# Transposing the third batch's q and k by DMA in place of TensorE

## Chip, cores, metric

One core of one Trainium2 chip. The metric is device time in microseconds (us) of one launch; the runs of the kernel before lie within 0.3% (316.71 to 317.66 us).

## The reference, cut to what matters

Sliding-window attention (window 32 to each side, 8 batches of 8 heads, 576 positions, head size 64), then a feed-forward layer with a smooth ReLU over all 4,608 positions.

```python
scores = scale * np.matmul(q, k.transpose(0, 1, 3, 2))      # q, k: [8, 8, 576, 64] float32
scores = np.where(np.abs(pos[:, None] - pos[None, :]) <= 32, scores, -1e9)
attn = softmax(scores); x = attn @ v                        # heads joined: [4608, 512]
h = x @ w_in; g = smelu(h); out = g @ w_out                 # 512 -> 2048 -> 512
```

## The kernel before

The kernel's score matmuls read q and k with the head's 64 values on the partitions (the lines `bb<-qT,kT 64*64` in the profiles), so each batch's q and k are transposed. The kernel has two ways. The first two batches after the start (numbers 1 and 2 in the code; number 2 is called the third batch below) are loaded in long runs and transposed by TensorE into PSUM, from where ACT and DVE copy them out. The later batches are loaded in natural rows of 64 values and transposed by one DMA per tensor, issued from SyncE.

```python
LONG = 3                       # batches 0..2 go through TensorE, 3..7 through DMA transposes
def load_rows(b, t):           # one DMA of 576 KB, runs of 1152 bytes at the destination
    x = nat.tile([128, NU, 2, D], BF, name=nm, tag=nm)           # pool "nat": two buffers a tag
    nc.gpsimd.dma_start(out=dst[b], in_=src[b].rearrange("(m e) (p j) d -> (e p) m (j d)", e=2, j=9))
def load_nat(b, t):            # two DMAs of 288 KB, runs of 128 bytes at the destination
    for h in range(2):
        nc.gpsimd.dma_start(out=x[:, :, h], in_=src[b, NY * h:NY * h + NY]...)
def tposes(b, *sets):          # TensorE: 36 transposes a tensor into the PSUM pairs "bb" ...
    for (t, half), pool in zip(sets, (ps_s, ps_n)):
        tp = pool.tile([128, 2, 8, 128], BF, name="tp", tag="bb")
        todo += [tpose(b, 2 * half + part, t, (A.copy, V.tensor_copy)[part], tp[:, part]) for part in range(2)]
    for copy in todo:          # ... and four copies out by ACT and DVE
        copy()
def xpose(b, t):               # DMA transpose
    nc.sync.dma_start_transpose(out=qkT(b, t)..., in_=(qn, kn)[t][b]...)
# [...]  loads are all issued on GpSimd, in order, as early as buffers allow:
put([(load_rows, 2, t) for t in range(2)] + [(load_v, 2, n) for n in range(4)])
# [...]  the slots
for n, a in enumerate((18, 20, 22, 27)):            at(a, seq[2 + n][0])    # sums
for n, a in enumerate((13.5, 14.5, 16, 18, 20, 25, 27)): at(a, seq[n][1])   # scores; n = 5: batch 2
for b, *a in ((1, 11.5, 12.5), (2, 19.5, 21.5)):    # slots of the TensorE transposes
    for t in range(2):
        at(a[t], (tposes, b, (t, 0), (t, 1)))
for b in range(LONG, B):                            # later batches: loads, then DMA transposes
    a = sl[5 * (b - 1) - 7] - 17
    ...
# [...]  one slot of the main loop:
#   hp (8 matmuls), ACT rr, DVE mx and gT;  run(a);  matmuls into op of an earlier tile;  run(a + 0.5);
#   then on SyncE the DMA transposes that are placed in this slot. Output stores are on SyncE too.
```

The softmax here doesn't subtract the row's maximum and nothing guards it: scores larger than these inputs give would overflow.

## Time and profile before

| | before |
|---|---|
| time, median | 316.87 us (316.71 to 317.66; three runs, a fourth makes it 316.85) |
| PE, DVE, ACT busy | 95%, 80%, 61% |
| DMA engines | busy 90% or more until about 110 us |

A line of the timeline is: start in us, duration in us, engine, source line, operation, written and read tiles, count; in brackets, the idle time of the engine before it and what ended it. The prediction below shows the lines of before and reads them. Its packet rates are in the packets' records of the same trace: about 840 packets of 256 bytes per us while a DMA transpose runs in quiet (414 to 427 per half us from 83.5 to 85.5 us), 84 to 92 long load packets per half us from 46.5 to 50 us, and 603 to 617 short ones from 59.5 to 62.5 us. The record of 219 to 220 ns that it names is that of one TensorE transpose.

### The profile page before, as it was taken

The numbers are of one execution on the slowest core, as the hardware profiler recorded it, in microseconds if no ns is written. First come the engines' busy times: TensorE is split into PE (matmuls) and PEld (weight loads), VectorE is DVE, ScalarE is ACT, GpSimd is POOL, SyncE is SP. The second block draws the span as 40 slices with busy tenths as digits, with TensorE's granted clock in tenths as the row PEclk, the third lists the DMA queues.
The fourth block names the chain that finished last, engine by engine and source line by source line (L and its number), as shares of the span: only waits on it lengthen the run. The fifth ranks groups of instructions, "written<-read, shape, count | busy, mean of one in ns | idle before, by whom it ended". The sixth has DMA issues, their size and how long they took to land.

```text
span 315.0 us, 8563 instructions
## 1 busy us (share of the span) xinstructions
PE 298.4 (95%) x3670; PEld 207.7 (66%) x3707; DVE 250.8 (80%) x393; ACT 192.1 (61%) x316; POOL 69.5 (22%) x83
## 2 busy tenths in 40 slices
PE   8987998999999999999999999999999999999995
PEld 3566877776666666666666666666666666667652
DVE  4279986877988888888888888888888888878760
ACT  3677375765765776567756666566676666654431
POOL 8784354652060406040503000000000000000000
PEclk9999999999999999999999999999999999999999
DMA  9999999999999969997993983005501100100111
GB/s 151 185 199 202 174 215 174 164 169 166 168 167 117 107 141 167 101 91 123 173 127 54 90 127 95 33 35 111 108 35 35 36 33 35 36 33 35 42 60 67
DMA packets 123558, 34.54 MB, mean 110 GB/s; under 512 B 108160, under 2 KB 119168, under 8 KB 123520
## 3 DMA queue, kind: packets, MB, share of 16 engines
q0 software_dynamic: 94176, 18.06, 74.1%
q1 hardware_dynamic: 29200, 15.63, 19.7%
q8 instruction: 29, 0.48, 0.6%
q10 hardware_dynamic: 144, 0.29, 0.4%
q14 instruction: 9, 0.07, 0.1%
HBM read 36.70 MB, written 9.44 MB: 146 GB/s over the span
## 4 chain that ended last, share of the span: by engine, by line
PE 86%; DVE 5%; ACT 5%; issue 3%; ACTq 0%
PE hp L484 37%; PE op L424 35%; PE bb L289 5%; PE op L440 4%; PE bb L223 2%; PE z L332 2%; DVE mx L490 2%; ACT pt L231 1%; ACT rc L296 1%; DVE gT L491 1%; PE tp L183 1%; DVE xT L301 1%; ACT lr L295 1%; DVE kT L186 1%; DVE qT L186 1%
## 5 line engine op out<-in xcount | busy, mean ns | idle before, releaser
L484 PE MATMUL hp<-xT,w_in 128*128 128x256 bf16 x1152 | 149.3, 273 | 4.0 <-DVE mx L490 1.9
L488 ACT ACTIVATE rr<-hp 128x512 f32<-128x512 f32 x144 | 85.7, 595 | 92.5 <-PE hp L484 91.1
L484 PEld LDWEIGHTS <-w_in 128*128 128x128 bf16 x1152 | 111.8, 98 | 44.2 <-issue 5.0
L424 PE MATMUL op<-w_out,gT 128*128 128x512 bf16 x477 | 123.0, 379 | 5.0 <-issue 4.8
L490 DVE TENSOR_TENSOR mx<-hp,rr 128x512 f32<-128x512 f32 x144 | 99.3, 690 | 33.7 <-ACT rr L488 31.5
L491 DVE SCALAR_TENSOR_TENSOR gT<-rr,mx 128x512 bf16<-128x512 f32 x144 | 99.6, 692 | 4.9
L424 PEld LDWEIGHTS <-gT 128*128 128x128 bf16 x512 | 47.6, 98 | 36.7
L231 ACT ACTIVATE pt<-bb 128x1024 bf16<-128x1024 f32 (+1 forms) x33 | 33.2, 1012 | 5.4 <-PE bb L223 4.0
L105 POOL DMA_DIRECT2D vn<-in_v_dram x32 | 27.3, 867 | 40.7 <-PE bb L223 36.2
L301 DVE TENSOR_TENSOR xT<-bb,rc 128x512 bf16<-128x512 f32 (+1 forms) x32 | 21.1, 658 | 11.1 <-ACT rc L296 10.4
L429 ACT COPY osb<-op 128x512 f32<-128x512 f32 x32 | 18.7, 583 | 11.5 <-PE op L424 11.1
L296 ACT ACTIVATE rc<-lr 128x512 f32<-128x512 f32 (+2 forms) x40 | 23.6, 589 | 1.3
L295 ACT ACTIVATE lr<-bb 128x512 f32<-128x512 f32 (+2 forms) x40 | 22.0, 551 | 0.8 <-PE bb L289 0.7
L97 POOL DMA_DIRECT2D qn<-in_q_dram x10 | 12.2, 1222 | 43.9 <-DMA qT<-qn 37.5
L289 PE MATMUL bb<-pt,ones 64*64 64x256 bf16 (+3 forms) x352 | 19.6, 255 | 1.9 <-DVE kT L186 0.8
L197 DVE TENSOR_TENSOR pt<-pt,mask 128x1024 bf16<-128x1024 bf16 (+1 forms) x34 | 21.0, 616 | 0.2 <-ACT pt L231 0.2
L289 PE MATMUL bb<-pt,vn 64*64 64x128 bf16 (+3 forms) x712 | 18.5, 204 | 0.2 <-issue 0.2
L289 PEld LDWEIGHTS <-ones 64*64 64x64 bf16 x352 | 10.4, 105 | 10.4 <-issue 10.4
L289 PEld LDWEIGHTS <-vn 64*64 64x64 bf16 x712 | 16.8, 107 | 0.3 <-issue 0.3
L440 PE MATMUL op<-w_out,gT 128*128 128x256 bf16 x128 | 16.3, 273 | 0.0
L97 POOL DMA_DIRECT2D kn<-in_k_dram x10 | 12.1, 1213 | 9.7 <-PE tp L183 3.9
L440 PEld LDWEIGHTS <-gT 128*128 128x128 bf16 x128 | 12.1, 98 | 1.7
(53 smaller groups left out, 107.8 us busy)
## 6 DMA issues: line engine op xcount, KB each, us to landing
out_dram<-osb SPq DMA_DIRECT2D x36, 256.0 KB, 2.3
vn<-in_v_dram POOLq DMA_DIRECT2D x32, 144.0 KB, 8.2
qn<-in_q_dram POOLq DMA_DIRECT2D x10, 288.0 KB, 7.7
kn<-in_k_dram POOLq DMA_DIRECT2D x10, 288.0 KB, 8.8
w_out<-in_moe_w_out_dram POOLq DMA_DIRECT2D x4, 512.0 KB, 13.2
qn<-in_q_dram POOLq DMA_DIRECT2D x2, 576.0 KB, 14.7
kn<-in_k_dram POOLq DMA_DIRECT2D x2, 576.0 KB, 15.7
w_in<-in_moe_w_in_dram POOLq DMA_DIRECT2D x8, 128.0 KB, 5.4
```

The costliest lines, as they stand in the source:

```text
L97: nc.gpsimd.dma_start(out=x[:, :, h], in_=src[b, NY * h:NY * h + NY].rearrange("y s d -> (y s) d") .rearrange("(u p) d -> p u d", p=128))
L105: nc.gpsimd.dma_start(out=vn[b][64 * a:64 * a + 64, :, h], in_=v[b, y:y + 2].rearrange("y s d -> (y s) d") .rearrange("(c r) d -> r c d", ...
L231: A.activation(p, ps[:, :, :128 * n].rearrange(like, y=m), AF.Exp, scale=D ** -0.5)
L289: nc.tensor.matmul(bb[HD[h], a, o + c0:o + c1], ones[HD[a]] if c is None else vn[b][HD[a], c, h], p(a, h), start=n == 0, stop=True, skip_g ...
L295: A.activation(lr[:, :, :D0], bb[:, :, D0:2 * D0], AF.Ln)
L296: A.activation(rc[:, :, :D0], lr[:, :, :D0], AF.Exp, scale=-1.0)
L424: nc.tensor.matmul(o, gT[tt // 2][:, j, 128 * (tt % 2):128 * (tt % 2) + 128], w_out[:, j], start=not done, stop=len(done) == 2 * NF - 1, s ...
L440: nc.tensor.matmul(o[:, tt], gT[p][:, j, 128 * tt:128 * tt + 128], w_out[:, j, 256 * half:256 * half + 256], start=not done, stop=len(done ...
L484: nc.tensor.matmul(hp[:, j], w_in[:, kk, 256 * f + 128 * j:256 * f + 128 * j + 128], xT[:, kk, r0:r0 + TB], start=n == 0, stop=n == 3)
L488: A.activation(rr, hp, AF.Relu, scale=0.5, bias=0.5)
L490: V.tensor_max(mx, hp, rr)
L491: V.scalar_tensor_tensor(gT[t][:, 2 * f:2 * f + 2], rr, 1.0, mx, op0=ALU.min, op1=ALU.mult)
```

## The change

The intent: 72 matmuls, their eight copies and two waits leave the busiest engine's row, and the DMA engines do the work instead, as they do for the later batches.

```diff
-    LONG = 3
+    LONG = 2
@@
-    put([(load_rows, 2, t) for t in range(2)] + [(load_v, 2, n) for n in range(4)])
+    put([(load_nat, 2, t) for t in range(2)] + [(load_v, 2, n) for n in range(4)])
@@
-    for b, *a in ((1, 11.5, 12.5), (2, 19.5, 21.5)):
-        for t in range(2):
-            at(a[t], (tposes, b, (t, 0), (t, 1)))
-    loads, xps = {}, {}
-    for b in range(LONG, B):
+    for t, a in enumerate((11.5, 12.5)):
+        at(a, (tposes, 1, (t, 0), (t, 1)))
+    loads, xps = {}, {17: [(2, 0)], 18: [(2, 1)]}
+    for b in range(LONG + 1, B):
```

## The prediction

> **What bounds the kernel now.** I read the page's busy shares and chain first: TensorE (PE) is busy 95% of the 315.0 us, and the chain that ended last is PE work for 86% of the span.
>
> ```profile
> PE 298.4 (95%) x3670; PEld 207.7 (66%) x3707; DVE 250.8 (80%) x393; ACT 192.1 (61%) x316; POOL 69.5 (22%) x83
> DMA  9999999999999969997993983005501100100111
> PE 86%; DVE 5%; ACT 5%; issue 3%; ACTq 0%
> ```
>
> So time is saved only by taking work out of PE's row, or the few waits inside it. The line in the middle (DMA, busy tenths in 40 slices) says that the transfers are busy in nearly all of the first third (a slice is 7.9 us, 9 is 90% or more), which is where the change adds transfers. Next I read the PE timeline around the work that goes. A "slot" is one turn of the main loop; each begins with eight matmuls of L484, so slots can be counted: 17 starts at 52.85 us, 19 at 57.25, 20 at 60.22, 22 at 66.54, 25 at 73.14.
>
> ```profile
> 58.12 1.04 PE L440 MATMUL op<-w_out,gT 128*128 128x256 bf16 x8
> 59.09 1.20 PE L183 MATMUL tp<-ident,qn 128*64 128x128 bf16 x36
> 60.22 1.05 PE L484 MATMUL hp<-xT,w_in 128*128 128x256 bf16 x8
> 62.03 0.30 PE L289 MATMUL bb<-pt,ones 64*64 64x256 bf16 x4 [0.77 <-DVE qT L186]
> ...
> 65.42 1.20 PE L183 MATMUL tp<-ident,kn 128*64 128x128 bf16 x36
> 66.54 1.05 PE L484 MATMUL hp<-xT,w_in 128*128 128x256 bf16 x8
> 68.36 0.28 PE L289 MATMUL bb<-pt,ones 64*64 64x192 bf16 x4 [0.77 <-DVE kT L186]
> ...
> 74.11 0.42 PE L223 MATMUL bb<-qT,kT 64*64 64x128 bf16 x16
> ```
>
> The second and fifth lines are the third batch's transposes (slots 19 and 21). Each is followed, one slot later, by a PE idle gap of 0.77 us: the sums need the PSUM pair "bb" that the transposes have filled, until DVE has copied it out. The last line is slot 25's scores, the first reader of the third batch's qT and kT: the deadline for whatever makes them.
>
> The deadline is then held against the transfers. The loads as they are, then an existing later transpose pair (fourth batch) and its landing:
>
> ```profile
> L91 POOL DMA_DIRECT2D qn<-in_q_dram x1: 754/754/754, 33.4 to 33.4; - x1
> DMA to landing us min/median/max: 15.9/15.9/15.9
> ...
> L91 POOL DMA_DIRECT2D kn<-in_k_dram x1: 742/742/742, 36.3 to 36.3; - x1
> DMA to landing us min/median/max: 15.8/15.8/15.8
> ```
>
> ```profile
> 40.30 32.29 SPq L446 DMA_DIRECT2D out_dram<-osb  x4
> 81.44 0.34 SPq L430 DMA_DIRECT2D out_dram<-osb  x1
> 81.96 2.89 SPq L190 DMA_TRANSPOSE qT<-qn  x1
> 85.01 2.41 SPq L190 DMA_TRANSPOSE kT<-kn  x1
> ```
>
> So q lands at 33.4 + 15.9 = 49.3 us and k at 36.3 + 15.8 = 52.1, and in a quiet stretch SyncE is occupied for 2.4 to 2.9 us by each transpose; the view of issues gives 4.9 us to landing for q and 4.7 for k.
>
> [...] 840 packets of 256 bytes per us while one runs, 215 GB/s. [...] here a record is 219 to 220 ns, but 36 issue in 1.13 us, 31 ns each, and that is what PE's row loses. [...] a 256 KB store issued at 52.9 us, amid loads, gets its first packet only at 57 us, and then loads fall from about 610 packets per half us to 130 to 200 beside the store's 95 to 99.
>
> **Removed.** 72 matmuls with 72 weight loads, in two runs: 60.22 - 59.09 = 1.13 us and 66.54 - 65.42 = 1.12 us of PE's row. The two PE waits after them, 2 x 0.77 = 1.54 us. Eight copies out of PSUM: DVE 4 x 0.72 = 2.9 us and ACT 4 x 0.76 = 3.0 us, beside PE and worth nothing more than the waits already counted. Sum on PE's row: 1.13 + 1.12 + 1.54 = 3.8 us.
>
> Does another wait step into the gap? The freed sums of slot 20 also need the earlier use of "bb" to be multiplied out by DVE, done at 59.4 us; without the transposes they are due at 59.1 + 0.9 = 60.0, so that holds. Stepping ACT's and DVE's order through slots 20 to 22 with their recorded durations, the next sums would be due at about 64.3 us, and their inputs at about 63.3; they stand at 68.36 now. That gives 4.0 us, the upper figure; I take 3.8.
>
> **Added: loads.** The third batch's q and k become four loads of 288 KB, in runs of 128 bytes at the destination, in place of two of 576 KB in runs of 1,152. From the packets' records in the saturated stretch: 90 long packets per half us, so 512 take 2.9 us; 610 short ones, so 2,304 take 1.9 us and a tensor (4,608) 3.8 us, 4.2 to 4.4 by the landings of the fourth batch. Extra: about 1.4 us per tensor, 2.8 us for both. The number of packets grows ninefold, but DMA time does not. In the program's order each load waits for the one eight before it; from the old landings I get q complete at about 51 us and k at about 55, and the values after them at about 60, needed in slot 27 (after 77 us now).
>
> **Added: transposes.** Two on SyncE, placed after the store at 52.87. q can start at about 53.3, k at about 56.2 (its load being in at 55). In quiet, landing would be 58 and 61 us. The stretch is not quiet: as with the store, about 3.5 us before the first packet, and then, at half of the 840 packets per us, 2,304 take 5.5 us. Estimated q lands at 62 to 63 and k at 67 to 68. The reader in slot 25, now at 74.1, will come at 74.1 - 3.8 = 70.3. So the transposes are hidden, with 2 us to spare in the slow case and 9 in the quiet one. No PE, DVE or ACT time is added. SyncE's next store is held up some us; its three output buffers bear that. The fifth batch's loads now wait for these transposes rather than for PE's; that moves them by a few us at most, and the transposes that use them run near 113 us.
>
> **Moved.** Everything after slot 22 moves forward by the same amount, if nothing later is tied to a transfer: the fourth batch's q and k have landed by 66 us and are transposed after 82, so there is room to lose the added 2.8 us and more.
>
> **Rivals.** (1) The transposes land late: amid saturated loads they take longer than I sized, and slot 25 waits. For it: the store's 7 us to landing there against 2.3 in the median. Against: 9 us of slack in quiet. It would give back what exceeds 70.3 us; k at 72 leaves 2 us of gain (315), at 75 none (317.5). (2) DVE or ACT becomes the bound where PE's row closes up, so that the gain is cut to the PE time alone, 2.25 us (314.6). For: DVE is busy 3.6 of the 4 us from 58 us on. Against: 1.35 us of that is a pair of the copies which go. (3) The extra load time pushes a later load past its need. Against it: the room above. It would cost 1 to 3 us. (4) Removing PE work moves the end by nothing, because transfers bound the stretch. Against: between 57 and 71 us the view of waits names a transfer only once on PE's side, for 0.2 us, at a weight load that goes.
>
> **Range and chances.** 316.87 - 3.8 = 313.1. The low end is the 4.0 us of the stepping plus some small luck, 312.2; the high end is the first rival with about 2.5 us given back, 315.4. Faster by over 2% needs 6.3 us, two thirds more than all that is removed: 0.02. Slower by over 2% needs the kernel to stall for 10 us at slot 25, beyond anything seen of HW transfers here: 0.03. The rest, 0.95, is within 2%.
>
> **What would show it.** In the trace after: no L183 lines with qn or kn after 45 us, 72 in place of 144 of them; no 0.77 us gaps at L289 with qT or kT copies as releasers; sums of slot 22 near 64.3 to 64.6 us; two DMA_TRANSPOSE on SyncE near 53 and 56 us, landing under 68; the L223 group of slot 25 without a wait for a transfer, near 70.3 us; the fifth batch's loads still well ahead. I am wrong if that group waits for a DMA_TRANSPOSE (rival 1), if new L484 or L289 waits for DVE stand between 58 and 70 us (rival 2), if a later load ends a PE wait (3), or if slot 25 starts earlier and the end does not (a later bound that I missed).

## The result, and the profile after

The changed kernel took 318.98 us in the median (318.45 to 319.50, four runs) against 316.85 (316.71 to 317.66) of the kernel before. The ratio is 1.0062 (95% interval 1.0037 to 1.0087). Ratios here are the mean time of one kernel's runs over the mean of the other's runs of the same rounds, so not quite the ratio of the medians. Timed again later beside other experiments (e9_again), it took 317.89 us, ratio 1.0035 (1.0007 to 1.0063). So it is one to two us slower, within 2% as forecast but outside the range of 312.2 to 315.4 us, and on the other side of the kernel before.

The page of the kernel after, its busy line, its clock and the chain by engine and by line:

```profile
PE 303.3 (96%) x3635; PEld 206.5 (65%) x3635; DVE 247.9 (78%) x388; ACT 189.1 (60%) x312; POOL 72.7 (23%) x85
PEclk9999999997999999999999999999999999999999
PE 75%; DMA 18%; POOL 4%; issue 1%; ACT 0%; POOLq 0%
```

PE has 35 fewer records: 72 matmuls are gone, but the trace before lacks 37 records, 35 of them of its L424 (477 of 512, 123.0 us busy against 131.3 here), so PE's busy times of the two pages can't be compared. One slice of the clock shows a 7. The chain now contains 18% of DMA, where the kernel before had none among its leading entries. Where that is, the timeline of PE in the kernel after tells:

```profile
58.94 1.04 PE L439 MATMUL op<-w_out,gT 128*128 128x256 bf16 x8
59.81 1.04 PE L483 MATMUL hp<-xT,w_in 128*128 128x256 bf16 x8
60.78 0.30 PE L289 MATMUL bb<-pt,ones 64*64 64x256 bf16 x4
...
65.03 0.28 PE L289 MATMUL bb<-pt,ones 64*64 64x192 bf16 x4
...
69.82 1.04 PE L483 MATMUL hp<-xT,w_in 128*128 128x256 bf16 x8
74.31 0.42 PE L223 MATMUL bb<-qT,kT 64*64 64x128 bf16 x16 [3.45 <-DMA kT<-kn]
74.66 1.47 PE L423 MATMUL op<-w_out,gT 128*128 128x512 bf16 x4
75.92 1.91 PE L483 MATMUL hp<-xT,w_in 128*128 128x256 bf16 x8
77.62 1.49 PE L423 MATMUL op<-w_out,gT 128*128 128x512 bf16 x4
78.95 1.04 PE L483 MATMUL hp<-xT,w_in 128*128 128x256 bf16 x8
```

The transposes and both 0.77 us gaps are gone: slot 22's sums start at 65.03 instead of 68.36 us. Then the scores of slot 25, ready to go just after 70.8 us, wait 3.45 us for kT. After the wait the same groups of matmuls take longer: 1.91 us for eight of L483 that take 1.04 elsewhere. The view by windows of the kernel after (start and end, length, busy us of each engine with instructions, granted PE clock, DMA share, GB/s) gives the reason:

```profile
70.00:74.00 4.00, 0.86 (x8) 0.52 (x6) 2.56 (x4) 0.60 (x1) 1.22 (x1) 1.00 1.78 167
74.00:76.00 2.00, 1.69 (x21) 0.81 (x22) 0.16 (x1) 1.02 (x1) 1.19 (x1) 0.78 1.43 258
76.00:78.00 2.00, 2.00 (x10) 1.29 (x9) 0.53 (x1) 0.08 (x1) 0.02 (x1) 0.50 2.43 155
78.00:80.00 2.00, 2.00 (x16) 1.16 (x18) 1.38 (x2) 0.51 (x1) 1.56 (x2) 0.86 2.51 158
```

The clock falls to a half (0.50). Its records put this from 75.13 us for 3.41 us, so about 1.7 us of work are lost. SyncE's timeline in the kernel after shows how kT came so late:

```profile
53.68 0.38 SPq L445 DMA_DIRECT2D out_dram<-osb  x1
54.18 7.29 SPq L190 DMA_TRANSPOSE qT<-qn  x1
61.57 6.81 SPq L190 DMA_TRANSPOSE kT<-kn  x1
```

Each transpose holds SyncE for about 7 us, not the 2.4 to 2.9 us of the quiet ones (nine of ten in the kernel before; one took 3.5), and the second is issued only when the first lets go. By the packets' records, q's 2,304 packets run from 59.53 to 65.96 us and k's from 66.81 to 72.95, at about 412 per us for most of that time, with an equal number of load packets beside them; the loads alone move about 1,200 per us. When SyncE lets go of q's transpose, at 61.47 us, only 633 of its packets have gone out: the hold is long, but it doesn't last for the whole transfer. kT has landed at 74.27 us.

To compare the traces slot by slot I take the start of DVE's last operation (gT) in each slot. Up to slot 19 the executions differ by -0.21 to +1.35 us against the profiled run of before, in most of them set before the first slot ends. The changed kernel stands at +0.82 in its first profile (its clock rose to full at 6.86 us, that of before at 5.18, and the 14 fillers at the start took 5.98 us against 5.15), +0.35 in its second, and at -0.19 and -0.21 in two experiments that share its early instructions (e6_early, e7_swap), so this belongs to the execution, and I subtract what slot 19 has. The end varies too: before and e1_none end 9.9 us after the last slot's gT starts, the other nine traces 10.3, with PE's last matmul at the same distance in all. From slot 19 on:

| us against before, less the difference in slot 19 | by slot 24 | by slot 27 | by slot 48 and to the last slot |
|---|---|---|---|
| changed kernel | -4.14 | +1.06 | +1.18 |

So 4.14 us were gained, and 5.20 lost again in two slots: 3.45 of waiting and about 1.75 of slow clock.

### The profile page after: what moved, and what is told of

Read it like the earlier page. It is cut to its first block, busy times and chain, and to the rows that moved or that the text cites.

```text
span 317.4 us, 8453 instructions
## 1 busy us (share of the span) xinstructions
PE 303.3 (96%) x3635; PEld 206.5 (65%) x3635; DVE 247.9 (78%) x388; ACT 189.1 (60%) x312; POOL 72.7 (23%) x85
## 4 chain that ended last, share of the span: by engine, by line
PE 75%; DMA 18%; POOL 4%; issue 1%; ACT 0%; POOLq 0%
PE op L423 36%; PE hp L483 33%; DMA kn<-in_k_dram 12%; PE bb L289 5%; DMA kT<-kn 4%; DMA qh<-in_q_dram 2%; PE bb L223 2%; POOL w_in L109 2%; POOL vn L105 1%; POOL w_out L114 1%; POOL qn L97 0%; POOL kh L84 0%; POOL qn L91 0%; ACT osb L428 0%; PE bb L248 0%
## 5 line engine op out<-in xcount | busy, mean ns | idle before, releaser
L483 PE MATMUL hp<-xT,w_in 128*128 128x256 bf16 x1152 | 150.1, 274 | 3.7 <-DVE mx L489 1.3
L483 PEld LDWEIGHTS <-w_in 128*128 128x128 bf16 x1152 | 112.4, 98 | 44.4 <-issue 5.1
L423 PE MATMUL op<-w_out,gT 128*128 128x512 bf16 x512 | 131.3, 382 | 0.0
L423 PEld LDWEIGHTS <-gT 128*128 128x128 bf16 x512 | 47.8, 98 | 37.2 <-issue 0.6
L97 POOL DMA_DIRECT2D qn<-in_q_dram x12 | 14.6, 1219 | 52.6 <-DMA qT<-qn 46.0
L97 POOL DMA_DIRECT2D kn<-in_k_dram x12 | 14.5, 1217 | 11.1 <-DMA kn<-in_k_dram 6.8
L223 PE MATMUL bb<-qT,kT 64*64 64x128 bf16 x520 | 13.0, 217 | 3.6 <-DMA kT<-kn 3.5
L289 PEld LDWEIGHTS <-ones 64*64 64x64 bf16 x352 | 10.3, 105 | 9.0 <-issue 8.9
```

Source lines behind the costliest of these rows:

```text
L289: nc.tensor.matmul(bb[HD[h], a, o + c0:o + c1], ones[HD[a]] if c is None else vn[b][HD[a], c, h], p(a, h), start=n == 0, stop=True, skip_g ...
L423: nc.tensor.matmul(o, gT[tt // 2][:, j, 128 * (tt % 2):128 * (tt % 2) + 128], w_out[:, j], start=not done, stop=len(done) == 2 * NF - 1, s ...
L483: nc.tensor.matmul(hp[:, j], w_in[:, kk, 256 * f + 128 * j:256 * f + 128 * j + 128], xT[:, kk, r0:r0 + TB], start=n == 0, stop=n == 3)
```

## The experiments

**Theory:** the gain on PE is real (4.1 us). kT is late because, beside saturated loads, a transpose gets every second packet (about 412 per us, to 412 of the loads), and the two run one after the other; and the wait for it costs more than its length, because the clock drops. **Rivals:** the load of k in small packets is what makes it late; or the cost lies elsewhere (packets, other engines) and the wait is only where it shows. The first rival is not idle, since the chain of waits of the kernel after, in order of time, reads:

```profile
39.22 14.47 DMA kn<-in_k_dram
...
54.38 7.19 DMA kn<-in_k_dram
61.57 12.70 DMA kT<-kn
74.31 0.42 PE bb L223 x16
```

It leads from kT to a load of kn. But the load that was issued at 54.38 us belongs to the fourth batch, and the third batch's k was in at 55.2 us (40.4 plus 14.8 by the view of its tile).

One thing stays open: none of the experiments tells whether the transposes run one after the other because SyncE is held or because packets keep their order in SyncE's queue. The packets speak for the queue. In the kernel before, k's transpose was issued at 85.01 us, while q's packets were going out, and its first packet came at 86.24, when q's last went; in the changed kernel only 0.85 us lie between q's last packet and k's first, and the hold can't have cost more if that order is kept.

### e1_none: no transposes at all

```diff
+    for t in range(2):
+        P.memset(qkT(2, t), 0.0)
-    loads, xps = {}, {17: [(2, 0)], 18: [(2, 1)]}
+    loads, xps = {}, {}
```

> Wrong result on purpose: the changed kernel, with the third batch's two DMA transposes left out and its qT and kT set to zero by GpSimd early. Loads as in the changed kernel. Theory (the loss comes from the wait of 3.45 us for kT in slot 25 and the lowered PE clock after it): both vanish and the 4.1 us that PE's row gained by slot 24 stays, so 316.85 - 4.1 = 312.7 us, no PE wait near slot 25, clock 1.0. Rival (the nine times as many load packets, or something else in the change, costs the time, and the wait is only where it shows): 316 us or more.

Measured: 313.24 us, 0.5 above what was expected, ratio 0.9881 (0.9868 to 0.9894), no PE wait near slot 25. It still passed the comparison with the reference: q and k are drawn so small that the scores are near zero anyway. By slot 24 it has gained 4.13 us and keeps 4.14 to the last slot. So the loads in small packets cost nothing at the end, and what PE's row gained is real; the loss comes from the transposes' lateness. 313.2 us is the mark for what the change could give.

### e2_warm: the same wait, with PE kept busy

```diff
+        if a == 25:
+            keep_warm(16, ps_h, "hp")
         run(a)
```

> The changed kernel with 16 matmuls of zeros (some 0.22 us each) in slot 25 ahead of the scores that wait for kT, so that PE is not idle in the wait. Theory (the wait lowers the granted clock for some 4 us, which costs about 1.7 us more): 318.98 - 1.7 = 317.3 us with clock 1.0; kT lands as before, near 74.3. Rival (the clock in the records is an effect without cost, or the extra 1.9 us after slot 25 come from elsewhere): no gain, 319 us or a little more.

Measured: 316.91 us, ratio 1.0000 (0.9988 to 1.0013), all five runs at clock 1.0. PE's timeline in this run:

```profile
69.93 3.62 PE L332 MATMUL z<-warm 128*128 128x512 bf16 x16
73.48 0.42 PE L223 MATMUL bb<-qT,kT 64*64 64x128 bf16 x16
73.83 1.04 PE L423 MATMUL op<-w_out,gT 128*128 128x512 bf16 x4
```

The fillers span the wait (kT landed at 73.24 us), and the next groups take 1.04 us, not 1.47 or 1.91. Of the 4.14 us gained by slot 24, 3.45 are given back and no more. So the slow clock is a cost of its own, and useless work in the wait removes it: one to two us by the two comparisons of the changed kernel with the kernel before.

### e3_gate: the next loads held back

```diff
+    gate = const.tile([128, 64], BF, name="gate")
@@
+        if a == 22:
+            P.tensor_copy(gate, gT[2][:, 9, 0:64])    # GpSimd waits for slot 20's gT, then loads batch 3
```

> The changed kernel with the fourth batch's loads held back on GpSimd by a small copy that reads what DVE makes in slot 20 (some 62 us); their wait is earlier in the changed kernel, at 50 us. Theory (a transpose runs at half rate because the loads in the queue take every second packet): SyncE is occupied 3 to 5 us by each transpose and not 7, kT lands before 70 us, slot 25 doesn't wait, about 313 us, unless the held loads then collide with the fourth batch's own transposes and make a wait in slot 39. Rival (a transpose takes 7 us here whatever runs beside it): SyncE 7 us each, kT near 74, 319 us.

Measured: 314.50 us, ratio 0.9921 (0.9907 to 0.9935), clock 1.0. SyncE's timeline in this run:

```profile
54.05 5.88 SPq L190 DMA_TRANSPOSE qT<-qn  x1
60.03 2.72 SPq L190 DMA_TRANSPOSE kT<-kn  x1
```

k's transpose is short again, and lands at 65.75 us (5.7 us after its issue, against 12.7 in the changed kernel), and slot 25 doesn't wait. q's hold is longer than the 3 to 5 us expected: loads issued before the gate still land until 59.95 us. So the length is not in the transpose but in what runs beside it. Of the 4.14 us gained, 0.91 were lost from slot 40 on: there the fourth batch's scores waited 0.7 us for kT, whose transposes (7.3 and 7.2 us on SyncE) ran beside loads that had been pushed back (the fifth batch's q and k landed from 84.7 to 100.1 us). A wait was moved and made smaller.

### e4_late: a later deadline

```diff
-    for n, a in enumerate((18, 20, 22, 27)):
+    for n, a in enumerate((18, 20, 22, 28.5)):
-    for n, a in enumerate((13.5, 14.5, 16, 18, 20, 25, 27)):
+    for n, a in enumerate((13.5, 14.5, 16, 18, 20, 26.5, 28.5)):
```

> The changed kernel with the third batch's first scores moved from slot 25 to 26.5 and its second scores and first sums from slot 27 to 28.5, transposes untouched. Theory (only the deadline in slot 25 is missed, by 3.5 us): the scores now come near 73.7 us, wait at most 1 us, too short to lower the clock; 313 to 314 us. Rival (the changed kernel is slower for another reason): 317 us or more.

Measured: 314.78 us, ratio 0.9928 (0.9914 to 0.9942). The transposes hold SyncE for 7.29 and 6.90 us as in the changed kernel, and kT lands at 73.81 us. The scores wait 1.08 us and the clock stays up (1.0 in this run, 0.999 to 1.0 in all six). 2.63 us of the gain are left: the wait and about 0.4 us that the new order costs. It came out about 0.8 us above the range expected. Only the deadline was moved, and the kernel went from slower than before to faster.

### e5_khalf: only k by DMA

```diff
-    put([(load_nat, 2, t) for t in range(2)] + ...
+    put([(load_rows, 2, 0), (load_nat, 2, 1)] + ...
+    at(19.5, (tposes, 2, (0, 0), (0, 1)))
-    loads, xps = {}, {17: [(2, 0)], 18: [(2, 1)]}
+    loads, xps = {}, {17: [(2, 1)]}
```

> Half of the change: only k is loaded in natural rows and transposed by DMA (in slot 17); q is loaded and transposed by TensorE as in the kernel before (slot 19). Theory (the second transpose is late because SyncE is occupied 7 us by the first): a single one is issued when its load is in, near 53 to 55 us, lands near 67 to 69, slot 25 (near 72) doesn't wait, and half of the gain of 4.1 us stays: 316.85 - 2.0 = 314.8 us. Rival (k is late because its load is late): kT lands near 74 again, a wait of 2 us or more, 317 us.

Measured: 315.50 us, ratio 0.9952 (0.9940 to 0.9963). k's transpose is issued at 54.26 us, holds SyncE for 6.74 us, as slow as ever, and lands at 68.40; slot 25 doesn't wait. The gain to the last slot is 2.06 us, half of 4.13, though the time is 0.7 us above the 314.8 expected. So one slow transpose is hidden; it is the second in the row that isn't.

### e6_early: both transposes ahead of slot 16's store

```diff
-    loads, xps = {}, {17: [(2, 0)], 18: [(2, 1)]}
+    loads, xps = {}, {15: [(2, 0), (2, 1)]}
```

> The changed kernel with both transposes placed in slot 15, ahead on SyncE of slot 16's store. Theory: q's transpose starts as soon as its loads are in (51.1 us, 3 us earlier), k's follows it at about 58.5 and lands near 71.3; the wait in slot 25 shrinks from 3.45 to under 1 us, the clock holds, 313 to 314 us. Rival (k is bound by its load or by the DMA queue's total work, not by SyncE's order): kT lands near 74 as before, 318 us or more.

Measured: 316.51 us, ratio 0.9960 (0.9936 to 0.9984), but spread from 314.50 to 316.96 over six runs. In the profiled run (316.96) k's transpose is issued at 58.46 and lands at 71.82, 2.5 us earlier than in the changed kernel, near what was expected. The wait, though, is 2.0 us and not under 1, because this execution's PE was 1.0 us earlier at the same point, and it was enough to bring one window of half clock (mean clock 0.994). Moving SyncE's order moved the landing, as the theory says; the expected time was missed. Of the other five runs one has 0.998 and four 1.0 at 314.5 to 316.9 us, so part of the spread may come from the length of the wait itself, which only the profiled run shows.

### e7_swap: k first, then q

```diff
-    loads, xps = {}, {17: [(2, 0)], 18: [(2, 1)]}
+    loads, xps = {}, {17: [(2, 1)], 18: [(2, 0)]}
```

> The changed kernel with the two transposes in the other order, k in slot 17 and q in 18. Theory (each occupies SyncE some 7 us while loads share the DMA engines): k starts near 55.2, when its load is in, q near 62.3, and the wait in slot 25 is now for qT, a little longer than 3.45 us; 319 to 320 us. Rival (k's load is what makes it late, as the chain of the changed kernel has it): with q free of it, q is issued within 3 us of k and the wait is gone or is for kT.

Measured: 321.03 us (two runs, 320.02 and 322.03), clock 0.989 in both, a little above the expected 319 to 320. SyncE's timeline, then PE's longest wait in the view of waits of this run (us in total, times, longest):

```profile
55.07 6.46 SPq L190 DMA_TRANSPOSE kT<-kn  x1
61.64 7.65 SPq L190 DMA_TRANSPOSE qT<-qn  x1
```

```profile
PE bb L223 <- DMA qT<-qn: 5.2, 1, 5.2
```

q's loads had landed at 50.6 us, and its transpose was still issued only when k's let SyncE go. The late one is whichever stands second. That refutes the rival of k's late load, and with it the chain's naming. The longer wait brought two windows of half clock, from 72.25 us for 6.83 us.

### e8_gates: every later batch's loads held back

```diff
+    gate = const.tile([128, 64], BF, name="gate")
-            loads.setdefault(a + t, []).append((b, t))
+            loads.setdefault(max(22, a - 5) + t, []).append((b, t))
@@
+            if x == 0:
+                c, g = divmod(a - 2, NF)
+                P.tensor_copy(gate, gT[c][:, 2 * g + 1, 0:64])
```

> As the run that held back the fourth batch's loads to slot 20, and every later batch's loads are held back too, until some slots after the transposes of the batch before (the fifth batch's to slot 32, near 87 us, and so on), so that no pair of transposes runs beside loads. Theory (transposes are slow only beside loads; the 0.7 us wait for kT in slot 40 of that run came from the fourth batch's transposes running beside the fifth batch's loads): every transpose occupies SyncE about 2.8 us, no PE wait for a transpose is left, and the whole 4.1 us stays: 316.9 - 4.1 = 312.8 us, at or under the run without transposes (313.2). Rival (the held loads come too late for their own use): a wait for vn, qT or kT after slot 55 and 314 us or more.

Measured: 313.97 us, ratio 0.9899 (0.9883 to 0.9915), the lowest of the versions that compute everything (its interval overlaps that of e3_gate), and faster than the kernel before and the changed one. SyncE's timeline in this run, the third and the fourth batch's transposes:

```profile
54.72 4.79 SPq L190 DMA_TRANSPOSE qT<-qn  x1
59.62 2.74 SPq L190 DMA_TRANSPOSE kT<-kn  x1
...
79.19 3.06 SPq L190 DMA_TRANSPOSE qT<-qn  x1
82.43 3.33 SPq L190 DMA_TRANSPOSE kT<-kn  x1
```

No PE wait for a transpose is left, and from slot 19 to slot 48 and on the gain is 4.14 us, all that e1_none had. The median is 0.7 us above that of e1_none and over the 312.8 expected. The two profiles differ by 0.92 us in span: 0.55 before slot 19 (+1.35 us here, +0.80 there), and 0.37 after the last slot's gT. These edits explain neither; it stays open.

### e9_again: the changed kernel's spread

> The changed kernel once more, for its spread beside the others. Theory: each run has one or two windows of half clock after the wait in slot 25, so a mean clock of 0.989 to 0.995 in all, and a median near 319.0 us. Rival (the lowered clock was chance): some runs at clock 1.0 and 317.3 us.

Measured: 317.89 us in the median of six runs, not the 319.0 expected, ratio 1.0035. The mean clock sorts the ten runs of both sessions: one run at 1.0 took 317.15 us; six at 0.993 to 0.995 took 317.55 to 319.21; three at 0.989 took 319.36 to 319.77. One window of 3.41 us at half clock is worth 0.5 x 3.41 / 317 = 0.5% of mean clock, so 0.995 is one window and 0.989 two. The rival had one run for it out of ten: the drop is usual, not certain. In the new profile the wait was 2.9 us, and there was one window.

The clock records also show where in time the waits that lowered it fell. In each of the four traces in which the clock fell in mid-kernel (the changed kernel twice, e6_early, e7_swap), it fell 68.27 us after it had risen to full at the start, which is 20 times 3.41. The other stretches of full clock in the records of before and of the changed kernel's first profile are such multiples as well: 310.61 us from the rise to the fall after the last instruction in before (91 times 3.413), and 238.93 us after the half clock in the changed kernel (70 times). I cut all eleven traces into stretches of 3.41 us from that rise on. The stretches that half clock followed in mid-kernel had PE idle for 2.01 to 2.77 us (2.60 and 2.49 in the changed kernel, 2.01 in e6_early, 2.42 and 2.77 in e7_swap), and no stretch that full clock followed had more than 1.74 (1.34 in before, 1.35 in the changed kernel's first profile). So in these traces a wait counts by how much of one stretch it fills. That one which is split over two can pass without a drop is my inference from them; it would explain the run at 1.0 here and the four of e6_early, but their traces weren't kept, so it isn't shown.

## Why the prediction was wrong

- **The bound and the removed work: right.** 3.8 us were forecast, 4.0 as the upper figure from stepping through the slots; 4.14 were gained by slot 24. Slot 22's sums started at 65.03 us; less the 0.82 of slot 19 that is 64.2, against 64.3 forecast. Neither DVE nor ACT stepped in (second rival wrong).
- **The loads: right where it mattered.** q was forecast complete at about 51 us and k at 55; they landed at 51.10 and 55.22. e1_none shows that the extra packets cost nothing.
- **The failed step: the landing, "k at 67 to 68".** That a transpose runs at half rate beside loads was my estimate (half of the 840 packets per us of the trace before), and it held (about 412); what it adds up to was sized too small, and kT landed at 74.27 us. The prediction doesn't write out how it came to 67 to 68. Its q comes to 53.3 + 3.5 + 5.5 = 62.3, and 5.5 more for k after q give 67.8. Against that sum, q was issued 0.9 us later (0.8 of it this execution's own start); the first packet came 5.35 us after the issue and not 3.5; q's packets took 6.43 us and k's 6.14, not 5.5 each; 0.85 us passed between q's last packet and k's first; and kT landed 1.32 us after its last packet, for which the sum has nothing. Together these are 6.5 us. The 3.5 us misreads their own source: the store issued at 52.9 had its first packet at 57, 4.1 us later. The deadline was 70.3 forecast, about 70.8 measured.
- **Also wrong: "k at about 56.2".** I let SyncE go after the quiet 2.9 us, while it was held for 7.29, so k was issued at 61.57, 5.4 us later. By the packets this can account for at most the 0.85 us above, if k's packets had to follow q's in any case.
- **The price of the wait: too low.** The first rival named the mechanism and priced k at 75 us as a gain of nothing, 317.5 us (its own numbers give 316.87 - 3.8 + 4.7 = 317.8). A wait was taken to cost its length. It also cost about 1.7 us for a window of half clock in which PE works (e2_warm avoids it).
- **The room of later batches: overrated.** "Moved" said that the fourth batch has room to lose more. Its transposes too ran beside loads (7.00 and 7.03 us on SyncE, kT landing at 104.5 us), and lost 0.12 us in slot 40; in e3_gate they lost 0.9.
- **The chances:** 0.95 for within 2% held, but the range's high end (315.4; 313.1 and the 2.5 us given back are 315.6) allowed the first rival only half of what it took.

## What to carry to other kernels

A transfer that takes work off the busiest engine has a deadline there; check it with the duration that such a transfer has in the same surroundings, from issue to landing (12.7 and 13.9 us here), not in a quiet stretch (4.6 to 4.9 us), and with the second starting after the first when two stand in a row. A wait on TensorE can cost more than its length: here the clock fell after 2.0 us or more of idle time within one stretch of 3.41, and not after 1.74 or less. Where DMA engines are saturated by loads that are needed much later, try holding those loads back: here that was worth more (314.50 and 313.97 us) than moving the late transposes forward (316.51).

## What the traces show of the DMA transposes and the clock

- SyncE is held for 2.4 to 2.9 us for 18 blocks of 128x128 in quiet (the fourth batch in the kernel before), and 6.8 to 7.3 us beside saturated loads (the third in the changed kernel); landing came 4.6 to 4.9 and 12.7 to 13.9 us after the issue.
- Beside the loads the packets went one for one in the changed kernel: about 412 packets of the transpose and 412 of the loads per us. In bytes that is unequal (256 against 128), and loads fall from about 1,200 packets per us to a third.
- A transpose's first packet came 1.3 us after its issue in quiet (81.96 to 83.29 in the kernel before, behind a store's packets) and 5.35 us beside loads, also behind a store's (54.18 to 59.53 in the changed kernel); with nothing ahead of it in SyncE's queue it was 4.7 us beside loads (e6_early, 50.59 to 55.29).
- Measured rate: 2,304 packets of 256 bytes in 2.95 us, 200 GB/s, in quiet (kernel before), and in 6.43 us, 92 GB/s, beside loads (changed kernel).
- Half clock lasted 3.41 us (changed kernel) or 6.83 us (e7_swap). Waits of 2.0 (e6_early) and 2.9 us (e9_again) brought a window of it, one of 1.08 us (e4_late) none; what separates the cases in these traces is the idle time within one stretch of 3.41 us, 2.01 us or more against 1.74 or less.
